# Talking-heads attention with an ELU feed-forward layer on one core: three edits to how the second block's scores are sent at the start

## The chip, the core and the metric

The kernel runs on one core of one Trainium2 chip. The metric is device time in microseconds (us), the median of several executions. The engines are TensorE (PE, with its weight loads as PEld), VectorE (DVE), ScalarE (ACT), GpSimd (POOL) and SyncE (SP). SP only issues transfers; POOL and ACT compute and can issue transfers too, each into a queue of its own. A core has 16 DMA engines, which all queues share. In the profile, SP's queue is q1 (hardware_dynamic) and POOL's is q0 (software_dynamic).

## The reference

```
# q, k, v: (batch 4, heads 12, positions 448, 64) float32;  w_pre, w_post: (12, 12)
scores = einsum('bhij,hg->bgij', (q @ k^T) / sqrt(64), w_pre)      # mix over heads
attn   = softmax(scores) over j, with 1e-9 added to the sum
attn   = einsum('bhij,hg->bgij', attn, w_post)                     # mix over heads again
x      = (attn @ v), heads side by side                            # (1792, 768)
out    = elu(x @ w_in) @ w_out                                     # 768 -> 2048 -> 768
```

## The kernel before, in words

**Tiling.** The attention works in blocks of query rows: four blocks for each of the four batches (`BLK`, L28), numbered n = 0 to 15. A block has up to 12 slots of ten rows. For each of the 12 heads PE multiplies queries with keys (`qk`, L208 on) and leaves a tile of 100 or 120 rows by 448 columns, one head at a time. The mix over heads needs another layout: all 12 heads of five rows side by side on 60 partitions. So each head's tile is copied out of PSUM by DVE or ACT (`keep_qk`, L224) and sent by a transfer from SBUF to SBUF into the block's raw buffer (`send`, L234): ten partitions, twelve apart, take twelve slots of 448 numbers (1792 bytes) each. Block 0 has ten slots, block 1 twelve. A whole send of 12 slots is 210 KB.

**Raw buffers.** There are two, `raws[0]` for even blocks and `raws[1]` for odd ones, each of 128 partitions by 12 x 448 numbers. Their first four partitions (`FRONT`) belong to no head but are read by PE with weights of zero, so they are cleared once: `raws[0]` by POOL at the very start (L326), `raws[1]` by POOL inside the loop (L401).

**Steps.** `scores` (L244) takes two slots of a raw buffer: PE multiplies them by the mixing weights `wa`, DVE finds the row maximum, ACT takes the exponential. `norm` (L263) makes the second mixing weights `wz` on POOL, `post` (L275) mixes on PE, `av` multiplies by v. The loop at L404 runs over steps j, two ahead with the scores (`LOOK` = 2): at j it issues scores of step j+2, then the sends that the step before left ready, attention times v, `qk` and `keep_qk` of a coming block, `post` of step j, and at last the planned work of j. Block 0 is steps 0 to 4, block 1 steps 5 to 10, block 2 begins with step 11. An engine takes its instructions in the order written, so this order is also the order on each queue.

**The start, before the loop (L324 to L358).** POOL clears the front of `raws[0]`. SP and ACT load keys and the queries of blocks 0 and 1. For block 0, PE makes the twelve heads' tiles; each is sent in two parts, first its first four slots (`FIRST`, so that scores can begin early), then after all heads the six others. SP sends the even heads of block 0 and POOL the odd ones (L238). Then the first eight heads of block 1 are made and sent, all by SP. In the loop, the last four heads of block 1 are made at j = 0, after the scores of step 2, and sent at j = 1. Block 2's queries are loaded by POOL in the planned work of j = -2 (L380), that is behind POOL's sends of block 0; there are two query buffers, so this load follows the use of block 0's queries. The clearing of `raws[1]`'s front stands behind it.

Of the kernel before, what the change touches and what calls it, by code (L numbers as in the profile page):

```python
# [22 lines left out]
FRONT = 64 - HR * H  # L23
# [88 lines left out]
@with_exitstack  # L112
def body(ctx, tc, qd, kd, vd, wpre, wpost, w1d, w2d, outT):
    xd = [[tc.dram_tile([128, NC, nt * R], F32, name=f"xd{b}_{i}") for i, (_, nt) in enumerate(BLK)]
          for b in range(B)]
    s1 = [tc.dram_tile([128, PW], F32, name=f"s1_{i}") for i in range(w1d.shape[0])]
    s2 = [tc.dram_tile([128, PW], F32, name=f"s2_{i}") for i in range(w2d.shape[0])]
    todo = [(d[i], s[i]) for d, s in ((w1d, s1), (w2d, s2)) for i in range(d.shape[0])]
    dec = Weights(tc.nc, ctx.enter_context(tc.tile_pool(name="dec", bufs=2, side="right")), todo, tc.nc.gpsimd)
    with tc.manual_schedule():  # L120
        moe = Moe(ctx, tc, xd, s1, s2, dec, outT)
        attention(tc, qd, kd, vd, wpre, wpost, xd, dec, moe)
        moe.run()
# [3 lines left out]
def attention(ctx, tc, qd, kd, vd, wpre, wpost, xd, dec, moe):  # L127
    nc = tc.nc
# [41 lines left out]
    raws = [rawp.tile([128, 12, S], F32, name=f"raw{i}") for i in range(2)]  # L170
# [6 lines left out]
    def load_k(b, hp, eng):  # L177
        k2[b, hp] = ld.tile([128, S], F32, tag="k2", name="k2", bufs=4)
        eng.dma_start(out=k2[b, hp], in_=kd[b, hp])

    def split_k(b, hp, high, low):
        src = k2.pop((b, hp))
        kh = kp.tile([128, S], F32R, tag="kh", name="kh")
        kl = kp.tile([128, S], F32R, tag="kl", name="kl")
        high(kh, src)
        low.tensor_sub(kl, src, f32(kh))
        ks[b, hp] = kh, kl

    def load_q(n, eng):
        q2[n] = ld.tile([128, NP, 120], F32, tag="q2", name="q2")  # L190
        eng.dma_start(out=q2[n], in_=qd[blocks[n]])

    def split_q(n, high, low):
        src = q2.pop(n)
        qh = qp.tile([128, NP, 120], F32R, tag="qh", name="qh")
        ql = qp.tile([128, NP, 120], F32R, tag="ql", name="ql")
        high(qh, src)
        low.tensor_sub(ql, src, f32(qh))
        qs[n] = qh, ql
# [7 lines left out]
    def qk(n, hp):  # L207
        m = slots[n] * R  # L208
        got = [bank("qk", six) for hh in range(2)]
        if n < 2:  # L210
            for hh in range(2):
                part = slice(hh * 64, (hh + 1) * 64)
                nc.tensor.matmul(  # L213
                    got[hh][:m, :S], q2[n][part, hp, :m], k2[0, hp][part], start=True, stop=True)
            return got
        (qh, ql), (kh, kl) = qs[n], ks[blocks[n][0], hp]
        for i, (q, k) in enumerate(((qh, kh), (qh, kl), (ql, kh))):
            for hh in range(2):
                part = slice(hh * 64, (hh + 1) * 64)
                nc.tensor.matmul(  # L220
                    got[hh][:m, :S], q[part, hp, :m], k[part], start=i == 0, stop=i == 2)
        return got

    def keep_qk(n, got, rooms=()):  # L224
        m = slots[n] * R
        out = []
        for hh, copy in ((1, nc.vector.tensor_copy), (0, nc.scalar.copy)):
            for hp, ps in got:
                st = rooms.pop() if rooms else stp.tile([120, S], F32, tag="st", name="st")
                copy(st[:m], ps[hh][:m, :S])  # L230
                out.append((2 * hp + hh, st))
        return out

    def send(n, out, t0=0, t1=None):  # L234
        t1 = t1 or slots[n]
        raw = raws[n % 2][:, t0:t1, :]
        for h, st in out:
            eng = nc.gpsimd if n == 0 and h % 2 else nc.sync  # L238
            lo = FRONT + h
            eng.dma_start(out=raw[lo:lo + (R - 1) * H + 1:H], in_=st[t0 * R:t1 * R])  # L240

# [82 lines left out]
    warm = pp.tile([128, S], F32, tag="p", name="warm")  # L324
    nc.vector.memset(warm, 0.0)
    nc.gpsimd.memset(raws[0][:FRONT], 0.0)  # L326
    k0 = atp.tile([128, NJ * 12 * RH], F32, tag="at", name="k0")[:, :NP * S].rearrange("p (h s) -> p h s", h=NP)
    q2[0] = ld.tile([128, NP, 120], F32, tag="q2", name="q2")
    nc.sync.dma_start(out=q2[0][:, 4:], in_=qd[0, 0][:, 4:])
# [19 lines left out]
    out = []  # L349
    for hp in (4, 5, 2, 3, 0, 1):  # L350
        got = keep_qk(0, [(hp, qk(0, hp))], rooms)
        send(0, got, 0, FIRST)
        out += got
    nc.vector.tensor_scalar_mul(wa, wa, 1.0 / float(np.sqrt(D)))
    send(0, out, FIRST)
    for hp in range(4):
        send(1, keep_qk(1, [(hp, qk(1, hp))]))
    rooms = [ld.tile([128, S], F32, tag="k2", name="room", bufs=4)[:120] for _ in range(4)]  # L358
# [3 lines left out]
    LOOK = 2  # L362
# [3 lines left out]
    def plan(j, f):  # L366
        work.setdefault(max(j, -LOOK), []).append(f)
# [6 lines left out]
    for n in range(1, NBL):  # L374
        b, i = blocks[n]
        at = [b * ROUND + j for j in (RAW_AT[i] if n > 1 else (0, 0, 0))]
        for u in range(2 if n == 1 else 0, 3):
            qks.setdefault(at[u], []).append((n, u))
        if n > 1:
            plan(3 if n == 3 else at[0] - 5, lambda n=n: load_q(n, nc.gpsimd))  # L380
        if n > 1:
            plan(at[0] - 2, lambda n=n: split_q(n, nc.vector.tensor_copy, nc.gpsimd))
        if i == (0 if b else 2):
            for hp in range(NP):
                t = at[hp // 2] - bool(b)
                if b:
                    plan(t - 5, lambda b=b, hp=hp: load_k(b, hp, nc.gpsimd))
                plan(t - 2 + hp % 2, lambda b=b, hp=hp: split_k(
                    b, hp, nc.vector.tensor_copy, nc.gpsimd))
# [8 lines left out]
    for hp in range(NP):  # L398
        plan((1, 2, 4, 5, 5, 6)[hp], lambda hp=hp: load_v(0, hp))

    plan(-LOOK, lambda: nc.gpsimd.memset(raws[1][:FRONT], 0.0))  # L401
    DENSE = {N - 3: (0, 0), N - 1: (0, 1), N: (1, 0), N + 1: (1, 1), N + 2: (2, 0)}
    sc, nz, ready = {}, {}, []
    for j in range(-LOOK, N + 3):  # L404
# [716 lines left out]
```

## Time and profile before

| | |
|---|---|
| median of 3 runs | 804.41 us (803.02 to 804.87) |
| the profiled execution, whole | 808.0 us |
| its span, first to last instruction | 806.2 us |
| PE busy | 770.4 us, 96% |
| DVE, ACT, POOL busy | 573.2, 509.9, 403.7 us |
| mean transfer rate | 217 GB/s |

The profiled execution is one run with the recorder on; its rows are in us from the start of its span. The chain of waits is the sequence of work that ended last, followed back from the last instruction; only what lies on it moves the end directly. The attention with its transfers takes about the first 350 us, the feed-forward layer the rest.

### The profile page before, as it was taken

To read this page: it belongs to the slowest core of one execution; us is meant where nothing else is said; L and a number is where in the kernel's file an instruction comes from. 1 tells how busy PE (TensorE), PEld (TensorE's weight loads), DVE (VectorE), ACT (ScalarE), POOL (GpSimd) and SP (SyncE) were. 2 spreads that over 40 slices of the span, in tenths; PEclk is the share of its full clock that TensorE was granted. 3 is DMA by queue.
4 is the path that set the end of the run, shared out by engine and by line. 5 is a ranking of instruction groups with operands and counts; after the bars stand their busy time and mean duration, and the time that the engine had idled before them with its cause. 6 is when DMAs were issued, how large, how long until landed. Compare 5 with 4: busy or idle time off the path is not lost.

```text
span 806.2 us, 25127 instructions
## 1 busy us (share of the span) xinstructions
PE 770.4 (96%) x10012; PEld 628.2 (78%) x10012; DVE 573.2 (71%) x1080; ACT 509.9 (63%) x1092; POOL 403.7 (50%) x527
## 2 busy tenths in 40 slices
PE   7589998989999999999999999999999999999998
PEld 2256666657666766678899999999999999999997
DVE  3657666867677667566999898777457777688962
ACT  4567877877777868784887883223157566665440
POOL 7656544654457353235788773275238787600000
PEclk9889999999999999999999999999999999999999
DMA  7648478865776675737999889987536768553331
GB/s 216 206 143 252 154 220 247 244 189 183 244 239 207 191 232 201 208 117 249 322 333 304 275 274 329 329 294 287 180 124 202 222 209 271 189 165 114 116 124 58
DMA packets 92908, 174.59 MB, mean 217 GB/s; under 512 B 21824, under 2 KB 59748, under 8 KB 92792
## 3 DMA queue, kind: packets, MB, share of 16 engines
q1 hardware_dynamic: 75576, 113.69, 43.7%
q0 software_dynamic: 16800, 58.61, 22.9%
q8 instruction: 79, 1.29, 0.7%
q10 hardware_dynamic: 416, 0.69, 0.2%
q14 instruction: 37, 0.30, 0.1%
HBM read 94.04 MB, written 39.35 MB: 165 GB/s over the span
## 4 chain that ended last, share of the span: by engine, by line
PE 89%; DMA 4%; issue 2%; ACT 1%; DVE 1%; SPq 1%; POOL 0%; ACTq 0%; DVEq 0%; POOLq 0%
PE y L689 14%; PE h L594 13%; PE y L1043 13%; PE h L981 13%; PE mixed L282 10%; PE xo L303 9%; PE s L251 8%; PE qk L220 7%; DMA raw<-room 2%; DMA raw<-st 2%; PE qk L213 1%; SPq L240 1%; ACT at L289 1%; DMA k<-in 0%; ACT p L258 0%
## 5 line engine op out<-in xcount | busy, mean ns | idle before, releaser
L256 DVE TENSOR_REDUCE nm<-s 128x1 f32<-128x448 f32 x180 | 103.9, 618 | 64.9 <-PE s L251 64.4
L258 ACT ACTIVATE p<-s,nm 128x448 f32<-128x448 f32 x180 | 112.8, 633 | 52.7 <-DVE nm L256 51.7
L271 POOL TENSOR_SCALAR wz<-wb,rz 128x60 f32<-128x60 f32 x180 | 78.6, 448 | 93.2 <-DVE rz L267 69.1
L289 ACT COPY at<-mixed 128x480 f32<-128x480 f32 (+1 forms) x184 | 93.4, 568 | 34.8 <-PE mixed L282 34.7
L282 PEld LDWEIGHTS mixed<-wz,p 64*64 64x64 f32 x5040 | 84.7, 135 | 36.1 <-issue 26.5
L251 PE MATMUL s<-raw,wa 64*64 64x448 f32 (+1 forms) x720 | 92.8, 560 | 18.0 <-DMA raw<-room 15.1
L282 PE MATMUL mixed<-wz,p 64*64 64x60 f32 x5040 | 98.6, 222 | 8.9 <-issue 7.5
L303 PEld LDWEIGHTS xo<-at,v 128*64 128x64 f32 x1536 | 75.9, 135 | 34.5 <-ACT st L230 22.6
L1043 PE MATMUL y<-part,hi 128*128 128x448 f32 x336 | 96.4, 367 | 0.0
L303 PE MATMUL xo<-at,v 128*64 128x120 f32 (+2 forms) x1536 | 87.0, 263 | 2.0 <-issue 2.0
L510 ACT CAST hi<-lo 128x1024 fp32r<-128x1024 f32 (+1 forms) x49 | 48.0, 980 | 40.8 <-PE y L1043 34.1
L981 PE MATMUL h<-op,hi 128*128 128x448 f32 x264 | 72.3, 367 | 0.0
L594 PE MATMUL h<-xh,hi 128*128 128x448 f32 x192 | 70.7, 368 | 0.0
L594 PE MATMUL h<-xh,lo 128*128 128x448 f32 x192 | 70.2, 366 | 0.3 <-POOL lo L511 0.3
L594 PE MATMUL h<-xl,hi 128*128 128x448 f32 x192 | 70.1, 365 | 0.0
L689 PE MATMUL y<-gl,hi 128*128 128x448 f32 x192 | 69.8, 364 | 0.0
L689 PE MATMUL y<-gh,hi 128*128 128x448 f32 x192 | 69.8, 364 | 0.0
L689 PE MATMUL y<-gh,lo 128*128 128x448 f32 x192 | 69.8, 363 | 0.0
L1043 PEld LDWEIGHTS y<-part,hi 128*128 128x128 f32 x336 | 63.0, 188 | 6.3
L981 PE MATMUL h<-op,lo 128*128 128x448 f32 x240 | 67.3, 367 | 0.0
L511 DVE TENSOR_TENSOR lo<-lo,hi 128x1024 fp32r<-128x1024 f32 x30 | 37.4, 1248 | 40.6 <-ACT hi L510 38.5
L1043 PE MATMUL y<-part,lo 128*128 128x448 f32 x168 | 61.8, 368 | 0.0
(119 smaller groups left out, 1636.1 us busy)
## 6 DMA issues: line engine op xcount, KB each, us to landing
raw<-st SPq DMA_DIRECT2D x140, 210.0 KB
w<-in POOLq DMA_DIRECT2D x48, 512.0 KB, 5.9
lo<-s SPq DMA_DIRECT2D x58, 256.0 KB
s<-c POOLq DMA_DIRECT2D x48, 256.0 KB, 6.0
raw<-st SPq DMA_DIRECT2D x36, 175.0 KB
v<-in POOLq DMA_DIRECT2D x24, 256.0 KB, 7.4
lo<-half SPq DMA_DIRECT2D x16, 384.0 KB
lo<-sum SPq DMA_DIRECT2D x12, 512.0 KB
```

Of the source, the lines that this page charges most:

```text
L220: nc.tensor.matmul(got[hh][:m, :S], q[part, hp, :m], k[part], start=i == 0, stop=i == 2)
L251: nc.tensor.matmul(ps[a][w * 64:(w + 1) * 64, :S], wa[half], raws[n % 2][half, ts[0] + w, :], start=True, stop=True)
L256: nc.vector.tensor_reduce(nm, ps[i][:, :S], op=ALU.max, axis=AX.X, negate=True)
L258: nc.scalar.activation(p, ps[i][:, :S], AF.Exp, bias=nm, scale=1.0, accum_out=z[:, i:i + 1])
L271: nc.gpsimd.tensor_scalar_mul(wz, wb, rz[:, i:i + 1])
L282: nc.tensor.matmul(mixed[w][half, i, c, :], p[part, j * 64:(j + 1) * 64], wz[part], start=True, stop=True)
L289: nc.scalar.copy(ats[n][:, :, ts[0]:ts[0] + len(ts), w, :], mixed[w][:, :len(ts)].rearrange("p t c n -> p c t n"))
L303: nc.tensor.matmul(ps[hh * 64:(hh + 1) * 64, w * m:(w + 1) * m].rearrange("p (t r) -> p t r", r=HR), vs[blocks[n][0], hp][:, c, hh * 64:(h ...
L594: self.nc.tensor.matmul(h, w[:, ks], x[:, k, :], start=n == 0, stop=n == 3 * NC - 1)
L689: nc.tensor.matmul(y[u], w[:, ks], g[f][:, u, :], start=f == 0 and n == 0, stop=f == NF - 1 and n == 2)
L981: nc.tensor.matmul(y, p[:, ks], x[:, z], start=q < 2 and k == 0 and n == 0, stop=k == KH - 1 and n == 2, skip_group_check=True)
L1043: nc.tensor.matmul(y, w[:, ks], g[:, x], start=begun is None and k == 0 and n == 0, stop=k == FH - 1 and n == 2, skip_group_check=True)
```

## The change

Three edits. The odd heads below 8 of block 1 (heads 1, 3, 5 and 7) are sent by POOL instead of SP. The front of `raws[1]` is no longer cleared by POOL's own instruction in the loop: a transfer issued by POOL right after `raws[0]`'s clearing copies the four cleared partitions over. The load of block 2's queries, still POOL's, is issued before the sends of block 1 instead of in the planned work of j = -2. Nothing of what is computed changes.

```diff
@@ send
-            eng = nc.gpsimd if n == 0 and h % 2 else nc.sync
+            eng = nc.gpsimd if h % 2 and (n == 0 or n == 1 and h < 8) else nc.sync
             lo = FRONT + h
             eng.dma_start(out=raw[lo:lo + (R - 1) * H + 1:H], in_=st[t0 * R:t1 * R])
@@ attention, the start
     nc.gpsimd.memset(raws[0][:FRONT], 0.0)
+    nc.gpsimd.dma_start(out=raws[1][:FRONT], in_=raws[0][:FRONT])
...
     send(0, out, FIRST)
+    load_q(2, nc.gpsimd)
     for hp in range(4):
         send(1, keep_qk(1, [(hp, qk(1, hp))]))
@@ attention, the planned work
-        if n > 1:
+        if n > 2:
             plan(3 if n == 3 else at[0] - 5, lambda n=n: load_q(n, nc.gpsimd))
...
-    plan(-LOOK, lambda: nc.gpsimd.memset(raws[1][:FRONT], 0.0))
```

## Rows read from the trace of the kernel before

**Rows 1.** The page's chain that ended last: share of the span.

```profile
PE 89%; DMA 4%; issue 2%; ACT 1%; DVE 1%; SPq 1%; POOL 0%; ACTq 0%; DVEq 0%; POOLq 0%
```

**Rows 2.** Waits, 0 to 110 us: engine, line, for what; total, times, longest.

```profile
PE s L251 <- DMA raw<-room: 15.1, 3, 8.2
```

**Rows 3.** Timeline of PE: start, us, what, then idle time before and its releaser.

```profile
23.31 1.33 PE L251 MATMUL s<-raw,wa 64*64 64x448 f32 x8 [3.11 <-DMA raw<-room]
...
32.93 1.40 PE L282 MATMUL mixed<-wz,p 64*64 64x60 f32 x56 [0.42 <-ACT at L289]
42.50 1.77 PE L251 MATMUL s<-raw,wa 64*64 64x448 f32 x8 [8.17 <-DMA raw<-room]
```

**Rows 4.** Chain of waits, 0 to 130 us: start, us, what.

```profile
15.22 2.42 SPq L240
...
19.27 3.80 DMA raw<-room
...
24.64 3.00 PE qk L213 x8
...
30.31 12.15 DMA raw<-room
...
42.50 1.77 PE s L251 x8
44.27 2.53 PE qk L220 x12
46.80 1.47 PE mixed L282 x56
...
58.28 1.42 PE qk L220 x12
59.70 0.97 PE mixed L282 x56
...
63.98 0.98 PE s L251 x8
```

**Rows 5.** Timeline of SP: start, us from first to last issue, what, count.

```profile
20.12 7.19 SPq L240 DMA_DIRECT2D raw<-st  x8
27.41 3.66 SPq L240 DMA_DIRECT2D raw<-room  x4
```

**Rows 6.** DMA queues, 20 to 33 us: packets, MB, share of 16 engines.

```profile
q1 hardware_dynamic: 1597, 2.62, 61.2%
```

**Rows 7.** DMA queues, 42.5 to 46 us.

```profile
DMA packets 47, 0.08 MB, mean 23 GB/s; under 512 B 5, under 2 KB 44, under 8 KB 47
...
q1 hardware_dynamic: 43, 0.07, 5.2%
```

**Rows 8.** DMA queues, 8 to 20 us.

```profile
q0 software_dynamic: 648, 1.42, 50.6%
q1 hardware_dynamic: 592, 0.75, 24.0%
```

**Rows 9.** Stretch 42 to 46 us: busy us by engine, granted clock, DMA share, GB/s.

```profile
42.00:46.00 4.00, 3.50 (x18) 1.89 (x20) 1.41 (x3) 0.95 (x3) 0.00 (x0) 0.50 0.06 25
```

**Rows 10.** Timeline of POOL.

```profile
6.90 0.72 POOL L240 DMA_DIRECT2D raw<-room  x1 [1.61 <-DVE room L230]
...
11.13 3.82 POOL L240 DMA_DIRECT2D raw<-room  x7 [0.21 <-DVE wa L354]
15.74 0.59 POOL L191 DMA_DIRECT2D q<-in  x1 [0.79 <-issue]
16.32 4.57 POOL L401 MEMSET raw<- 4x5376 f32 x1
21.23 0.85 POOL L271 TENSOR_SCALAR wz<-wb,rz 128x60 f32<-128x60 f32 x2 [0.35 <-DVE rz L267]
```

**Rows 11.** DMA issues, 0 to 45 us: size of one, median us to landing.

```profile
raw<-room POOLq DMA_DIRECT2D x6, 105.0 KB, 5.0
```

**Rows 12.** Instructions of L240, 0 to 31.5 us, POOL's sends.

```profile
DMA to landing us min/median/max: 2.7/4.8/5.7
```

**Rows 13.** Chain of waits, 268 to 318 us.

```profile
271.21 2.79 DMA raw<-st
...
305.93 8.33 DMA raw<-st
```

## The prediction, made before the changed kernel ran

> **What bounds the kernel now.** I first read the page's chain that ended last: PE holds 89% of it and transfers only 4% [rows 1]. So an edit to transfers can pay only where PE stands still for one. The list of waits, kept to the first 110 us, finds the place: PE waited three times for sends into the raw buffer, 15.1 us in all, the longest 8.2 us [rows 2]. PE's timeline dates the two that matter here. At 23.31 the scores of step 2 come after 3.11 us idle: they need the last six slots of block 0. At 42.50 the scores of step 5 come after 8.17 us: they are the first to read block 1 [rows 3]. PE had finished its work before that at 32.93 + 1.40 = 34.33.
>
> The chain shows what leads up to each. To 23.31: SP's issues of block 0's second parts, one of them lasting 2.42 us, then 3.80 us from the last issue at 19.27 to landing. To 42.50: the last send of block 1, issued at 30.31, landed 12.15 us later [rows 4]. SP issued eight sends of block 1 from 20.12 and four from 27.41 [rows 5].
>
> Why 12 us? From 20 to 33 us q1 ran practically alone: 2.62 MB in 13 us, about 200 GB/s, at 61.2% of 16 engines, which is the share of ten engines kept full; a send writes ten partitions [rows 6]. Twelve sends of 210 KB are 2.6 MB, so 13 us of work from 20.12 on, done near 34 to 36 if the engines finished together. They did not: between 42.5 and 46 us q1 still moved 0.07 MB at 5.2% of the engines [rows 7], the share of one engine working off its backlog alone. The stall is a queue of sends whose slowest engine is late.
>
> PE also came back slow. From 42 to 46 us its granted clock was 0.50, that is 1.2 of 2.4 GHz, after the idle stretch [rows 9].
>
> **The change part by part.**
>
> *The stall at step 5: -8.17 at most.* If block 1 has landed when PE gets there, the whole 8.17 us go [rows 3]. *The clock behind it: -2.4.* The three pieces at half clock took 1.77, 2.53 and 1.47 us; the same pieces later take 0.98, 1.42 and 0.97 [rows 4]. The difference is 0.79 + 1.11 + 0.50 = 2.40.
>
> *SP.* Eight sends in 7.19 us are 0.90 each [rows 5]; four fewer free 3.6 us of SP. That alone is worth nothing: the last four heads wait for PE's `qk` of 24.64 to 27.64 [rows 4], so they still leave from about 27.4 and end near 31. What counts is that q1 has 860 KB less in front of them, some 4.3 us at 200 GB/s [rows 6].
>
> *What is left of the stall: +1.2.* The last send leaves at about 30.3 relative to PE's arrival at 34.33. A send into raw took 2.79 us to land at one place of the chain and 8.33 at another [rows 13]; landing at 33.1 leaves no stall, at 38.6 one of 4.3. I take 1.2, nearer the empty queue, since only four SP sends and what POOL sent long before stand ahead; some lag of the slowest engine stays.
>
> *Block 0's second parts: +2.0.* This is what the edit costs. POOL is free at 16.32 and issues at 3.82 / 7 = 0.55 us each [rows 10], so its four sends enter q0 from 16.3 to 18.5, in the stretch in which the path runs through SP's sends of block 0 (15.22 to 23.07 in rows 4). From 8 to 20 us, with both queues on sends, q0 took 1.42 MB and q1 only 0.75 [rows 8]: q1 comes second. Now q0 stays full some 4 us longer. The floor is zero: the last part lands 3.80 us after its issue as before; a gain is excluded, as nothing ahead of these sends is taken away. The ceiling: landing takes 5.7, the most of POOL's sends in this stretch [rows 12], instead of 3.80, and SP has one more issue of 2.42 instead of the usual 0.75 [rows 4]: 1.9 + 1.7 = 3.6. With POOL's median for parts of this size, 5.0 [rows 11], it is 1.2 without such an issue and 2.9 with one; I take 2.0, between them.
>
> *Zeros by transfer: +0.4.* It leaves POOL at about 5.3, in the 1.61 us that POOL idles before its first send at 6.90, and costs an issue of 0.55 to 0.72 [rows 10]. It lands long before step 5. If it delays a key load or the first send, that costs up to the 0.72; if not, nothing. I take 0.4. The clearing of 4.57 us that goes was hidden: POOL's next work waited for DVE until 21.23 anyway, 0.35 us after the clearing [rows 10]. In its place stand four issues, 2.2 us, so POOL is ready earlier, near 18.5, unless the sends must wait for older ones; `wz` is what queues behind them, with 2.7 us of cover.
>
> *Queries in front: 0.* On POOL the load followed block 0's sends directly at 15.74 and still does [rows 10]. Without this edit it would stand behind four more sends, 2.2 us; its first reader is behind that.
>
> *Denser transfers afterwards: +1.0.* The 8 us pause let the slow engine drain [rows 7]. Without it block 2's sends and the loads of v meet a queue not yet empty. Block 2's scores at 63.98 wait for nothing now [rows 4]; the bounds are 0 and the 2.79 to 8.33 of later waits [rows 13]. I take 1.0 and keep the rest as a rival.
>
> *Sum:* -8.17 - 2.40 + 1.2 + 2.0 + 0.4 + 1.0 = -5.97, call it -6.0. The profiled execution took 808.0 (span 806.2 and 1.8 around it), so 802.0 there. The median of the runs is 804.41, 3.6 below it; the same 6.0 off gives **798.4**. Its own range, from the terms at their bounds, is 795 to 801.5.
>
> **The rivals.**
>
> *A. Another queue adds no bandwidth.* The two queues together moved 1.42 + 0.75 = 2.17 MB in 12 us, 181 GB/s [rows 8], not more than q1 alone [rows 6]. Then block 1 gains only its earlier start: 16.32 for 20.12 [rows 5, 10], 3.8 us; it is complete at 38.7. PE starts there instead of 42.50, the slow clock stays, and 0.4 + 1.0 are paid: -2.4, so 802.0. Against it: with the ten engines of q1 the limit, q0's packets may fall on idle ones. The Trainium skill, "DMA: Bandwidth & Descriptors", section "Issuing engines are not separate DMA queues", says just that transfers from all issuers share the same 16 engines, and that a second issuer only saves issue time; the trace agrees on the rate. The same page, "Why a DMA increments its semaphore by 16 and not by 1", says SP's transfers take the lowest-numbered engines while POOL's rotate over all; no row here tells engines apart. By the first rule the sum would be A's, by the second the forecast's.
>
> *B. The stall moves to block 2.* With the pause gone, the sends of block 2 come on top of the backlog, and step 11 waits between 2.79 and 8.33 us, mean 5.6 [rows 13]. Of 6.0 nothing is left but 0.4: 804.0. For it: the backlog lasted till 46 [rows 7]. Against: block 2's later sends cross the loads of v today too, and step 11 doesn't wait [rows 4].
>
> *C. Slower: the price at block 0 is paid and the stall stays.* Eight sends of block 1 still go through q1's ten engines, the last one's 12.15 us [rows 4] being the slowest engine's, not the queue's. If landing after the last issue shrinks by less than block 0's second parts are late, everything from 23.31 on shifts: +2.0 + 0.4, so 806.8, and with the ceiling of 3.6 some 808.4. It decides where the last landing is still over 10 us behind its issue. Against: a third of the queue is gone.
>
> *D. It doesn't do what it says.* POOL's sends wait for older ones to land (0.79 us idle stood before 15.74 already [rows 10]) and enter q0 so late that they end with SP's. Then 804.4.
>
> **How the numbers follow.** Forecast 0.42, A 0.22, B 0.14, C 0.16, D 0.06. A measurement can tell about 0.2%, 1.6 us, from no change: faster is below 802.8, slower above 806.0. Faster: nearly all of the forecast's 0.42, 0.15 of A, 0.05 of B: 0.62. Slower: 0.13 of C, 0.03 of B, 0.01 of D: 0.17. The rest, 0.21, is no change. The range is 795 to 806.2: it takes in the forecast's good end, A, B and D, and leaves out some 0.05 below and 0.14 above.
>
> **What would show it.** The idle time before step 5's scores falls from 8.17 to under 3 us and the clock behind it stays at 1.00. The scores of step 2 start near 25.5 instead of 23.31. POOL's four sends stand between 16 and 19 us. SP has four issues where eight stood, and `wz` is not late. Block 2's scores still follow PE without a wait. The prediction is wrong if step 2 is more than 4 us late, if the wait of 8 us is still there, or if it turns up at step 11.

## The result and the profile after

The changed kernel is slower: 810.39 us against 804.74 in runs beside it, 22 of each. The medians differ by +5.65 us where -6.0 was forecast, the means by +4.70. The ratio is 1.0079 with a 95% interval of 1.0053 to 1.0104. Ratios, here and below, leave out the slow runs, those more than 1.5% above the fastest of their kernel, while medians take in all, so the two can differ. 810.39 lies above the range of 795 to 806.2. The profiled execution took 812.2, its span 810.4.

Page of the changed kernel, the chain that ended last [rows 1]. Transfers hold 8% of it, where it was 4%; but this share goes with the execution (9% in before_again, 4% in after_beside, both below).

```profile
PE 84%; DMA 8%; issue 3%; ACT 2%; DVE 2%; SPq 1%; POOL 0%; ACTq 0%; POOLq 0%; DVEq 0%
```

Waits of the changed kernel, 0 to 110 us [rows 2], the two of PE's scores:

```profile
PE s L251 <- DMA q<-in: 8.1, 1, 8.1
...
PE s L251 <- DMA raw<-room: 3.5, 1, 3.5
```

Its PE timeline [rows 3]: the scores of steps 0 and 1, of step 2, of step 5 and of step 11, block 2's first.

```profile
21.25 3.27 PE L251 MATMUL s<-raw,wa 64*64 64x448 f32 x16 [8.08 <-DMA q<-in]
28.04 1.77 PE L251 MATMUL s<-raw,wa 64*64 64x448 f32 x8 [3.53 <-DMA raw<-room]
...
40.44 0.98 PE L251 MATMUL s<-raw,wa 64*64 64x448 f32 x8 [0.20 <-issue]
...
61.78 0.98 PE L251 MATMUL s<-raw,wa 64*64 64x448 f32 x8
```

Step 5 does not wait for transfers here, as forecast. But PE stands still earlier: the first scores start at 21.25 instead of 16.93, and step 2's at 28.04 instead of 23.31. (The releaser of the first is inferred; what PE reads there are block 0's first parts.) The clock behind step 5 stays up, 1.00 where it was 0.50 [rows 9]:

```profile
42.00:46.00 4.00, 3.49 (x90) 2.03 (x89) 3.63 (x9) 3.39 (x9) 2.67 (x5) 1.00 0.75 253
```

The chain of the changed kernel up to step 2 [rows 4]:

```profile
18.18 0.75 SPq L240
18.98 2.04 SPq L240
21.06 2.84 SPq L240
23.94 3.86 DMA raw<-room
```

From the last issue to landing it takes 3.86 us, as before (3.80). The last issue itself leaves at 23.94, not 19.27: SP is what is late. SP's timeline [rows 5]:

```profile
6.53 18.16 SPq L240 DMA_DIRECT2D raw<-room  x12
24.79 3.33 SPq L240 DMA_DIRECT2D raw<-st  x4
32.32 3.96 SPq L240 DMA_DIRECT2D raw<-room  x4
```

POOL's timeline [rows 10]: the zeros leave at 5.60, the queries at 16.50, the four sends from 17.11 to 19.47. `wz` waits for DVE, not for the sends.

```profile
5.60 0.69 POOL L327 DMA_DIRECT2D raw<-raw  x1 [0.31 <-POOL raw L326]
...
16.50 0.60 POOL L191 DMA_DIRECT2D q<-in  x1
17.11 2.36 POOL L240 DMA_DIRECT2D raw<-st  x4
25.57 0.85 POOL L271 TENSOR_SCALAR wz<-wb,rz 128x60 f32<-128x60 f32 x2 [6.09 <-DVE rz L267]
```

### The profile page after: what moved, and what is told of

It reads as the page before. It is cut to its first block, busy times and chain, and to the rows that moved or that the text cites. A ratio compares the mean times of both kernels' runs of the same rounds, so it can differ in the third digit from the quotient of the medians.

```text
span 810.4 us, 25133 instructions
## 1 busy us (share of the span) xinstructions
PE 773.5 (95%) x10012; PEld 630.1 (78%) x10012; DVE 578.0 (71%) x1080; ACT 509.5 (63%) x1092; POOL 408.1 (50%) x531
## 4 chain that ended last, share of the span: by engine, by line
PE 84%; DMA 8%; issue 3%; ACT 2%; DVE 2%; SPq 1%; POOL 0%; ACTq 0%; POOLq 0%; DVEq 0%
PE y L690 14%; PE h L595 13%; PE y L1044 13%; PE h L982 13%; PE mixed L282 8%; PE xo L303 8%; PE s L251 7%; DMA raw<-st 7%; PE qk L220 6%; PE qk L213 2%; SPq L240 1%; ACT at L289 1%; ACT p L258 1%; DMA raw<-room 0%; DMA k<-in 0%
## 5 line engine op out<-in xcount | busy, mean ns | idle before, releaser
L89 ACT ACTIVATE sq<-w 128x512 f32<-128x512 f32 x48 | 32.1, 669 | 48.2 <-DVE c L94 38.9
```

## The experiments

**Is the wait of 8.17 us the kernel's?** The kernel before, unchanged, profiled twice more.

> The kernel before once more, for a second profile. Theory 3 (the wait of 8.17 us before step 5 was an accident of the profiled execution, one DMA engine late): the wait is under 4 us here. If it belongs to the kernel, it is 6 to 10 us again.

> The kernel before, a third profile. Theory 3 (the wait of 8.17 us before step 5 is an accident of single executions): under 2 us here, as the 0.43 of the second profile; step 2's scores at 23 to 24. If it comes and goes half of the time, 4 to 10 us.

PE's timeline of before_again (the first scores, steps 2, 5 and 11), and steps 5 and 11 of before_third:

```profile
18.16 3.27 PE L251 MATMUL s<-raw,wa 64*64 64x448 f32 x16 [5.35 <-DMA raw<-room]
23.12 1.77 PE L251 MATMUL s<-raw,wa 64*64 64x448 f32 x8 [1.70 <-DMA raw<-st]
...
34.40 0.98 PE L251 MATMUL s<-raw,wa 64*64 64x448 f32 x8 [0.43 <-DMA raw<-room]
...
56.21 0.98 PE L251 MATMUL s<-raw,wa 64*64 64x448 f32 x8
```

```profile
34.80 0.98 PE L251 MATMUL s<-raw,wa 64*64 64x448 f32 x8 [0.93 <-DMA raw<-room]
...
56.42 0.98 PE L251 MATMUL s<-raw,wa 64*64 64x448 f32 x8
```

The same program waits 0.43 and 0.93 us at step 5, and the clock there is 1.00 in both (34 to 38 us). Of six executions in which block 1 leaves by SP as before (these three, and copy_only, copy_beside and queries_late below) one has the long wait. It was an accident of the execution that was profiled, one engine working off a backlog [rows 7], not a cost of the kernel. Nor does the wait decide how long an execution takes: 808.0 us with it, 812.55 (before_again) and 797.11 (before_third) without. Where does the difference between these two lie? Windows of both, 0 to 60 us and 60 to 350 us: behind the length stand PE's busy time with its matmuls in brackets, the same of the other engines, PE's granted clock, the busy share of the DMA engines and GB/s.

```profile
0.00:60.00 60.00, 48.89 (x840) 26.87 (x840) 36.75 (x82) 36.90 (x93) 42.91 (x62) 0.91 0.74 224
60.00:350.00 290.00, 270.74 (x6598) 187.53 (x6594) 196.20 (x482) 214.85 (x545) 138.84 (x241) 0.97 0.68 206
```

```profile
0.00:60.00 60.00, 48.49 (x838) 26.49 (x840) 36.71 (x82) 36.63 (x93) 42.72 (x61) 0.91 0.76 226
60.00:350.00 290.00, 278.43 (x6946) 195.68 (x6939) 204.82 (x503) 226.42 (x575) 143.97 (x248) 1.00 0.68 207
```

The start is the same; behind 60 us PE is busy 7.7 us less in before_again, and the chain there has two transfers of 10.81 and 11.92 us, at 119 and 131 us. From 60 to 350 us PE's scores wait 12.0 us for sends in before_again and 3.2 in before_third: such waits come and go all along the attention.

**The changed kernel again.**

> The changed kernel, a second profile. If its late start belongs to the kernel: first scores at 20 to 22, step 2's at 27.5 to 31, step 11's row maximum 4 to 7 us behind that of the kernel before without its accident (57.2). If the first profile was chance, step 2 under 26.

> The changed kernel once more, beside the sends alone early, the same sends late and the copy alone, on one chip. Theory (early sends take the engines from block 0's second parts, the copied zeros from its first parts): 1.006 to 1.010 of before, step 2's scores start at 28 to 32 us. Rival (the cost is not in the start; any build differs by some us through later waits): between 0.997 and 1.005, with step 2 as late.

after_again took 810.25 us. after_beside, on one chip with three others (sends_early_beside, copy_beside and sends_late_beside below): 811.91 against 803.34, ratio 1.0104 (1.0044 to 1.0163). Steps 2 and 11 of after_again:

```profile
31.65 1.77 PE L251 MATMUL s<-raw,wa 64*64 64x448 f32 x8 [8.61 <-DMA raw<-st]
...
63.17 0.98 PE L251 MATMUL s<-raw,wa 64*64 64x448 f32 x8
```

The same two windows of after, after_again and after_beside:

```profile
0.00:60.00 60.00, 45.32 (x718) 24.14 (x719) 34.67 (x74) 34.00 (x85) 39.34 (x61) 0.86 0.69 207
60.00:350.00 290.00, 272.35 (x6748) 188.73 (x6750) 199.77 (x491) 218.22 (x555) 141.30 (x245) 0.98 0.69 211
```

```profile
0.00:60.00 60.00, 42.53 (x664) 22.12 (x668) 33.28 (x71) 31.37 (x79) 37.77 (x58) 0.86 0.67 193
60.00:350.00 290.00, 276.69 (x6855) 191.75 (x6850) 202.39 (x499) 222.12 (x567) 142.29 (x249) 0.99 0.70 214
```

```profile
0.00:60.00 60.00, 44.50 (x700) 23.46 (x700) 34.30 (x73) 33.42 (x84) 39.33 (x61) 0.86 0.69 203
60.00:350.00 290.00, 276.04 (x6944) 192.42 (x6940) 204.92 (x503) 225.40 (x573) 143.64 (x250) 0.99 0.69 212
```

In the first 60 us PE does 664 to 718 matmuls at a clock of 0.86, where the two executions of before without the accident do 838 or 840 at 0.91 (the one with it: 628 at 0.86). Behind 60 us it is busy 275.0 us in the mean, which is also the mean of the three of before (275.86 in the first), though single executions differ by up to 7.7. So what repeats lies in the start. Step 11's scores start at 61.78, 63.17 and 61.13 us, against 56.21 and 56.42 in the two executions of before without the accident: +5.7 us, the size that was measured. (With the accident, 63.98 [rows 4].) That the whole +5.65 is this delay is argued from the size, not shown: further on single executions scatter by more, and the last scores of the attention start between 337.66 and 353.08 us in the three of before, between 345.84 and 352.45 in the three of the changed kernel.

**Which edit?** Each one alone.

```diff
 sends_only, sends_early_beside:  the edit in send() alone
+            eng = nc.gpsimd if h % 2 and (n == 0 or n == 1 and h < 8) else nc.sync
 copy_only, copy_beside:  the zeros alone
+    nc.gpsimd.dma_start(out=raws[1][:FRONT], in_=raws[0][:FRONT])
-    plan(-LOOK, lambda: nc.gpsimd.memset(raws[1][:FRONT], 0.0))
 zeros_by_dve:  the whole change, but
-    nc.gpsimd.dma_start(out=raws[1][:FRONT], in_=raws[0][:FRONT])
+    nc.vector.memset(raws[1][:FRONT], 0.0)
```

> The kernel before with one edit: heads 1, 3, 5, 7 of block 1 sent by POOL; the clearing in the loop and the place of the query load stay. Theory 1: first scores at 16.9 as before, step 2 later than 23.3 by 1 to 3, the time from 4 us faster to 1 us slower. Theory 2: first scores at 16.9, step 2 at 27 or later, the time 4 to 6 us over the kernel before.

> The kernel before with one edit: the zeros of the second raw buffer by the transfer, POOL's clearing in the loop gone. Theory 1 (the transfer of four whole partitions keeps a few DMA engines busy for 7 us and holds up block 0's first sends): the first scores start at about 21 instead of 16.93, the scores of step 2 at about 27 instead of 23.3, and the time is 4 to 6 us over the kernel before. Theory 2 (POOL's four sends of block 1 hold up block 0, rival C of the prediction): first scores at 16.9 to 17.3, the time within 1 us of before.

> The changed kernel with the transfer of zeros replaced by a clearing on VectorE at the start; POOL's sends and the query load stay as changed. Theory 1: first scores at 17 to 18 instead of 21.25, the time 4 to 6 us under the changed kernel, at or under the kernel before. Theory 2: the time stays within 1.5 us of the changed kernel's 810.

> Only the four sends by POOL at about 16 to 19 us. Theory: step 2's scores at 28 to 31 us against some 23 of before, 1.006 to 1.012. Rival: as the others, between 0.997 and 1.005.

> Only the zeros by transfer. Theory: first scores 1.5 to 3 us late, 1.002 to 1.005. Rival: within 0.2% of before, since the first scores only wait a little longer and later waits take it up.

The sends alone: 814.11 us, 1.0137 (1.0077 to 1.0197), and beside the others 810.73, 1.0103 (1.0050 to 1.0157). The copy alone: 807.13 beside a median of 804.90, 1.0055 (1.0015 to 1.0095), and 807.25 beside 803.34, 1.0058 (1.0015 to 1.0100). zeros_by_dve: 809.0 beside 804.90, 1.0031 (0.9987 to 1.0075), which tells nothing by its time; its step 2 starts at 30.18 with the first scores on time at 17.30. On one chip the medians are +7.4 for the sends, +3.9 for the copy and +8.6 for the whole. The intervals, about half a per cent to either side, are too wide to say whether the two add up in the time. At step 2 they do not: the mean delay against the three of before is 8.0 us with the sends alone and 6.5 with both.

PE's timeline of sends_early_beside: the first scores are on time, step 2's are 8.4 us later than the 23.31 of before [rows 3].

```profile
16.70 2.68 PE L251 MATMUL s<-raw,wa 64*64 64x448 f32 x16 [3.37 <-DMA raw<-room]
31.68 1.77 PE L251 MATMUL s<-raw,wa 64*64 64x448 f32 x8 [12.30 <-DMA raw<-st]
...
44.15 0.98 PE L251 MATMUL s<-raw,wa 64*64 64x448 f32 x8 [0.20 <-issue]
```

In copy_only it is the other way round: the first scores start at 19.61, step 2's at 24.52. SP's timeline of copy_only, 6 to 13.5 us: three issues, where the kernel before has seven, which take 7.89 us.

```profile
6.52 7.26 SPq L240 DMA_DIRECT2D raw<-room  x3
```

**Is it the queue, the number, or the time at which they leave?** Two sends (heads 1 and 3) instead of four; four by ACT; four by POOL, but behind the first `wz`.

```diff
 sends_half
+            eng = nc.gpsimd if h % 2 and (n == 0 or n == 1 and h < 4) else nc.sync
 sends_by_act
+            eng = nc.gpsimd if n == 0 and h % 2 else nc.scalar if n == 1 and h < 8 and h % 2 else nc.sync
 sends_late, sends_late_again, sends_late_beside:  sends_only, and
-        send(1, keep_qk(1, [(hp, qk(1, hp))]))
+        got = keep_qk(1, [(hp, qk(1, hp))])
+        send(1, got[1:])
+        late += got[:1]
...
+    plan(-1, lambda: send(1, late))
```

> The kernel before with heads 1 and 3 alone sent by POOL: two sends instead of four. If the price grows with the bytes that come between (about 1.8 us for each send of 210 KB, from 30.4 against 23.3 with four), step 2's scores start at 26 to 27.5. If it is a fixed cost of having POOL's queue busy then, they start at 29 or later.

> The kernel before with heads 1, 3, 5, 7 of block 1 sent by ACT, whose queue is a hardware queue as SP's. If starting these sends early is what costs, step 2's scores start at 27 to 30 here too. If POOL's queue is what costs (its longer packets taking the engines), they start at 23 to 25.5.

> The kernel before with POOL's four sends of block 1 issued after POOL's first wz instead of right behind block 0's sends (about 24 us instead of 16). Theory 2 (the price is the overlap of these sends with block 0's second parts): step 2's scores at 23 to 24, the wait before step 5 under 2 us, the time within 2 us of the kernel before. Rival (any four sends by POOL cost, wherever they stand): step 2 or step 5 later by 4 or more, the time at 810 or above.

> The same kernel as sends_late, a second profile. In the first its feed-forward matmuls followed each other every 207 ns, in most other kernels every 200, 5 us over the whole. If this belongs to the compiled program, 207 again and about 463 us from the end of the scores to the end; if to the execution, 200 and 458 to 459.

> The same four sends by POOL, issued at about 26 us, behind the second mixing weights of the first step. Theory: step 2's scores at 23 to 25 us and at least 3 us less than the early sends, 1.000 to 1.004. Rival (POOL's sends cost later too, whenever they leave): no less than the early ones, 1.006 to 1.012.

sends_half took 808.38 and sends_by_act 805.91 us, one run each, beside a median of 801.25. With two sends step 2 starts at 28.58: between what was expected of a price by bytes (26 to 27.5) and of a fixed one (29 or later). Half the bytes cost +5.6 us over the mean of before (one profile), where all four cost +7.4 and +8.7, so the price does not follow the bytes alone. With ACT's queue step 2 is as late as with POOL's; ACT's sends leave earlier, from 11.27 us on, and the first scores are late too. PE's timeline of sends_by_act:

```profile
19.71 3.26 PE L251 MATMUL s<-raw,wa 64*64 64x448 f32 x16 [6.92 <-DMA raw<-room]
30.94 1.77 PE L251 MATMUL s<-raw,wa 64*64 64x448 f32 x8 [7.97 <-DMA raw<-room]
```

sends_late_beside, POOL and then PE: the four sends leave at 25.61, and step 2 is on time.

```profile
25.61 2.38 POOL L240 DMA_DIRECT2D raw<-st  x4
```

```profile
17.00 3.27 PE L251 MATMUL s<-raw,wa 64*64 64x448 f32 x16 [4.15 <-DMA raw<-room]
23.10 1.77 PE L251 MATMUL s<-raw,wa 64*64 64x448 f32 x8 [2.83 <-ACT p L258]
...
36.12 0.98 PE L251 MATMUL s<-raw,wa 64*64 64x448 f32 x8 [0.87 <-DMA raw<-room]
```

It took 805.92 us, 1.0048 (1.0008 to 1.0088). The median is 4.8 us less than that of the same sends early on that chip; the intervals of the two ratios overlap, and it is the timeline that decides. In the other two profiles step 2 starts at 24.39 and 23.80, and step 11 at 56.95 and 57.63 (56.25 here), near the 56.2 and 56.4 of before. So the price at step 2 depends on when the sends leave: it is paid where they leave before or among block 0's second parts, on whichever queue. Sent late they gain nothing either; block 1 was not late to begin with. The other two runs: 807.59 beside 801.25, 1.0084 (1.0043 to 1.0124), over the 2 us that were expected, and 805.81 in one run beside a median of 804.56.

What is left of +0.5 to +0.8% with step 2 on time is not explained by the start. For sends_late its profile places some 5 us: from the last scores to the end it takes 463.1 us (counted from their start) where the three of before take 457.6 to 457.7. In the feed-forward layer PE does 583 matmuls from 480 to 600 us instead of 598 or 599. sends_late_again, the same kernel, does 599, so the slower pace does not come from the edit; where it comes from is open. The profiles of sends_only and zeros_from_rows show it too (584 and 583), and their +1.4 and +1.6% may hold 5 us that are not the price of their edits.

**Why does a copy of 84 KB hurt?** Its shape: four partitions of 21.5 KB. zeros_from_rows is the whole change with the zeros read from 48 rows of 1792 bytes.

```diff
-    nc.gpsimd.dma_start(out=raws[1][:FRONT], in_=raws[0][:FRONT])
+    nc.gpsimd.dma_start(out=raws[1][:FRONT], in_=warm[:12 * FRONT])
```

> The changed kernel with the zeros read from 48 partitions of a cleared tile, 1792 bytes each, instead of four rows of 21504 bytes. Theory 1 (four long packets of 3.4 to 4.8 us keep four engines from block 0's first sends): packets under 1 us, first scores at 16.9 to 18.5 instead of 21.25, step 2 still near 28 to 30, the time 0 to 4 us under the changed kernel. Rival (the four cleared partitions are slow to write in any cut): first scores at 20 to 21.5.

Transfers from 5 to 14 us, after and then zeros_from_rows: four packets of after are not under 8 KB, and the last column of the issue is the time to landing.

```profile
DMA packets 1302, 1.86 MB, mean 207 GB/s; under 512 B 569, under 2 KB 1101, under 8 KB 1298
...
raw<-raw POOLq DMA_DIRECT2D x1, 84.0 KB, 7.5
```

```profile
DMA packets 1550, 2.17 MB, mean 241 GB/s; under 512 B 645, under 2 KB 1330, under 8 KB 1550
...
raw<-warm POOLq DMA_DIRECT2D x1, 84.0 KB, 6.5
```

With rows, 2.17 MB move instead of 1.86 and the first scores start at 16.74, on time. So it is the shape that holds up block 0's first parts, four packets of 21.5 KB that take 3.9 to 4.7 us each. (One profile; the copy from rows also leaves some 0.35 us earlier.) The price of the sends stays (step 2 at 30.07, behind 10.07 us idle): 813.28 us beside 801.25, 1.0160 (1.0105 to 1.0216). The 0 to 4 us under the changed kernel that were expected do not show in the time.

**The load of queries.** queries_late is the kernel before with the clearing of `raws[1]` (4.57 us) ahead of the load.

```diff
+    plan(-LOOK, lambda: nc.gpsimd.memset(raws[1][:FRONT], 0.0))   # ahead of the loop over load_q
-    plan(-LOOK, lambda: nc.gpsimd.memset(raws[1][:FRONT], 0.0))   # behind it
```

> The kernel before with POOL's clearing of the second raw buffer put ahead of the load of block 2's queries, so that the load (360 KB) leaves at about 20.3 instead of 15.7, behind block 0's second parts. Theory 2 (each 210 KB that any queue puts between block 0's sends delays step 2 by about 1.8 us): step 2's scores 1.5 to 3 us earlier, at 20.5 to 22, and the time 0 to 2 us under the kernel before. If POOL's load does not disturb SP's sends, step 2 stays at 23.1 to 23.3.

806.18 us, 1.0008 (0.9960 to 1.0056), step 2 at 21.64 and step 5 at 34.90: the load's place, 3.4 us later than 15.74, may bring step 2 forward by 1.4 us (one execution, against a mean of 23.0), but is worth nothing that can be measured in the time. No version was faster than the kernel before.

## Why the prediction was wrong

*The stall and the clock (-8.17, -2.40, +1.2).* This is the step that failed. The wait was read rightly in its execution, but it was taken for a property of the kernel on the strength of that one. In the next two it was 0.43 and 0.93 us, with the clock at 1.00. There was under 1 us to gain, not 9.4. So the 0.20 us and the clock of 1.00 in the changed kernel are no success of the edit: the unchanged kernel shows much the same. A sign was there: rows 7 show a single engine's share behind 42.5 us, which asks for a second profile. The other number at hand, the median 3.6 us below the profiled execution, was none, since before_again took 812.55 without the wait.

*Block 0's second parts (+2.0, bounds 0 to 3.6).* The mechanism was right, the size was not. Step 2 starts at 28.04, 31.65 and 28.95, mean 29.5, against 23.31, 23.12 and 22.60, mean 23.0: +6.5, where +2.4 was forecast with the zeros. The sends alone make it 30.41 and 31.68. Two things come together, SP's issues and the landing. Long issues were not new: the chain of before has two, one more than the prediction names.

```profile
11.94 2.44 SPq L240
```

The other is the 2.42 at 15.22 [rows 4]. The ceiling allowed one more. The changed kernel has four in its twelve: two of 3.43 and 2.48 us from 7.74, beside the copy, and the 2.04 and 2.84 beside block 1's sends. The twelve take 18.16 us, where they took 13.53. In the profile of after that is all: the last issue is 4.67 us later, landing as long as before. In sends_half the issues end only 1.3 us later, and landing makes up the rest. The semaphore counts in the trace show more. In every profile with POOL's four sends early, step 2 starts 0.24 or 0.25 us after SP's last part of block 0 has landed. Nine of the ten engines that carry this part end it between 27.5 and 28.9 us in all seven, and at 27.5 in sends_half (between 22.2 and 22.7 in the three of before). In three of the seven the tenth ends 2.5 to 4.0 us behind the nine, which is most of the spread between 28.04 and 31.68.

The engines show the contention. Transfers from 20 to 28 us, after and then before_third:

```profile
q0 software_dynamic: 347, 0.96, 47.0%
q1 hardware_dynamic: 599, 0.94, 39.4%
```

```profile
q1 hardware_dynamic: 1071, 1.75, 63.0%
q0 software_dynamic: 6, 0.01, 0.4%
```

While PE waits for block 0, POOL's queue, block 1's sends above all, takes half of what the engines do, and q1 gets 0.94 MB through instead of 1.75. The total hardly grows: 1.91, 1.61 and 1.74 MB in the three executions of the changed kernel, 1.59, 1.70 and 1.78 in the three of before, while the engines' busy share rises from between 61 and 64% to between 86 and 88%. So q0 does find engines that q1 leaves idle, but few more bytes arrive. Counted as bytes ahead of the work that PE needs first, the four sends are 0.86 MB at some 200 GB/s [rows 6], an estimate of +4.3 at step 2, nearer than the 2.0 but still too small; for sends_half it gives 2.2 where 5.6 was measured, so the bytes alone do not give the price. The Trainium skill, "DMA: Bandwidth & Descriptors", section "Issuing engines are not separate DMA queues", says that transfers of all issuers run on the same 16 engines and that a further issuer saves only issue time; these totals agree, and so does sends_by_act (1.34 MB). Rival A applied that rule to block 1 alone. Issue time was not saved here but lost: 18.16 us for SP's twelve instead of 13.53.

*Zeros by transfer (+0.4, bounds 0 to 0.72).* Too small: only the issue was priced, not what the transfer does to SP's sends beside it. The first scores start at 19.61 and 21.97 with the copy alone and at 21.25, 19.77 and 21.49 in the changed kernel, against 16.93, 18.16 and 18.02 before: +1.9 to +4.3 over the mean of before, 17.7. In the whole the copy alone costs 0.55 to 0.58% by the ratios, +2.2 and +3.9 us by the medians.

*Queries in front (0).* Nothing speaks against it; the edit alone changes no order in the kernel before and was not run.

*Denser transfers later (+1.0).* Not seen: PE's busy time from 60 to 350 us has the same mean, and step 11 starts without a wait.

*The range.* The forecast's own upper end of 801.5 does not follow from its terms: with 4.3 us left of the stall, 3.6, 0.72 and 1.0 the sum is -0.95, so 803.5, and with 8.33 for denser transfers instead of 1.0 it is 810.8. What was measured lies just inside the bounds that the terms had.

*The signs.* Right were POOL's sends between 16 and 19 us (17.11 to 19.47), SP's four issues, `wz` not held up by POOL, and, for a reason that was not the edit's, step 5. Wrong was step 2, 4.7 us late, over the 4 that were named.

*The rivals.* C has the right side and half the mechanism: the price at block 0 is paid, at more than its ceiling (806.8 to 808.4 were given, 810.39 measured). The stall did not stay; on most executions there was none. B's move to step 11 did not come, and D's late sends did not either (they left from 17.11).

*Left open.* How the +5.65 divides: sends and copy overlap, and the copy alone and the late sends cost more in the whole than their first 60 us show (copy_only starts step 11 at 56.09, no later than before). Why SP's issues grow long beside other queues' transfers no profile shows; that the engines' backlog does it is inferred. One profile cannot place 3 us where executions of the kernel before take anything from 797.89 to 815.07 us.

## What to carry to other kernels

A wait in one profiled execution is worth its length only if a second profile of the same kernel shows it. Where executions scatter by more than the gain that is sought, profile the kernel twice before a sum rests on one wait. And a send that is started earlier is not free on another queue: ask which transfer PE waits for at that moment. Counting the bytes put ahead of it, at the rate of all engines together, is a start, but it said too little here: two sends cost 5.6 us and four 7.4 and 8.7, where the bytes said 2.2 and 4.3.

## What was not expected of the hardware

- A copy of four partitions of 21.5 KB took 7.5 us to land, and SP, beside it, made three issues in 7.2 us instead of six or seven. The same 84 KB in 48 rows let SP go at its usual pace.
- Some of SP's issues took 2 to 3.9 us instead of 0.75 while another queue's transfers were under way: two in the first profile of the kernel before, four in that of the changed one. ACT's, in sends_by_act, took up to 2.28. Issuing is part of what contention costs.
- In the execution first profiled one DMA engine ended each send of block 1 later than the last, by up to 6 us behind the other engines (from the semaphore counts of the transfers in the trace); in the two others of the same program the slowest engine was under 1 us behind.
